# A fused attention and long-convolution kernel: zero products on TensorE at the start, shorter spectrum scaling, and a new order of small steps

## The chip, the cores and the metric

The kernel runs on one core of a Trainium2 chip. Its time is device microseconds (us) from launch to end, lower is better; the kernel before takes 284.23 us (median of 3 runs, 284.17 to 284.6). The engines are named as in the profile: PE is TensorE's matrix products (PEld its weight loads), DVE is VectorE, ACT is ScalarE, POOL is GpSimd, SP is SyncE, which here only issues DMAs. Each engine works its instructions off in the order in which they were written, and waits for the others by semaphores.

## The reference

Two parts, one behind the other. The first is block-sparse attention over 4 batches of 8 heads, 768 positions, 64 channels:

```python
k_rep = k.reshape(B, H, 12, 64, D).mean(axis=3)          # block means of the keys
gate  = einsum('bhsd,bhnd->bhsn', q, k_rep)               # causal blocks only
# each query sees its 3 best blocks and its own block, causally
attn  = softmax(mask(q @ k.T / sqrt(D)))
out   = attn @ v
```

The heads are laid side by side (512 channels) into `x`, and the second part is a gated convolution:

```python
x1, x2, x3 = split(x @ w_proj, 3)
x2_conv = irfft(rfft(x2) * rfft(filter))    # along the 768 positions
y = (x1 * x2_conv * x3) @ w_out
```

## The kernel before, in words

A head (32 in all, n = 0 to 31) is worked in three slots s = 0, 1, 2. A slot issues, in the order written: `scores(n, s)` (L464, products of queries and keys into a two-bank PSUM tile `sps`, then the exponential on ScalarE, L467); in slot 1 `normalise(n - 1)` (L505, L506 on VectorE); in slot 2 of even heads `turn_outputs` (L516, PE turns two heads' outputs `xn` into `xp`, and ScalarE copies them, L518); the stores of finished rows; `diagonals` (L475, Pool zeroes what lies above the diagonal); what the previous slot's unit left for later (`todo`, mostly two products or sums on Pool: L574 and L575 for `PQ`, L612 and L613 for `yT`); `prepare(n, s)` for later heads; `setup`; the units of the convolution of a batch that is finished; and at the end `product(pn, ps)` of the slot before (L490, exponentials times values). Since the order of each engine is the order of writing, it is this sequence that sets what waits behind what.

`prepare` readies heads to come. Up to head 11 queries and keys are cast, and turned on PE (`turn_pe`, L395, copied out at L397 by ScalarE or VectorE); from head 12 they are turned by a DMA on SP's queue (`turn_query`, L384), which waits until `low_query` (L379, Pool) has written the queries' low half from the remainder `rem` that VectorE takes (L375, in `query_rest`). `gate` makes the choice of blocks: products `gps` on PE (L414), then VectorE from L417 to L427 (`ga`, `g`, `m`, `get`, `gm`), and `turn_mask` (L438, L440) turns the result into twelve rows of the queries. Block sums of the keys come from PE for heads below 12 (`key_sums_mm`, L275; `key_sums_copy`, L282 and L284; `key_sums_turn`, L291; `key_sums_split`, L305 and L307). For heads 12 to 31 they come from three lists in `by_block`: DMAs on Pool's queue that add the keys up in memory (`add_blocks`, L319, tile `k_blk`; the last number of each list says in which heads' slot 2 they are issued), a fold and sums on VectorE (`fold_blocks`, L325; `sum_blocks`, L331 and L335, tile `krb`), a turn on PE (`turn_blocks`, L340, tile `krt`) and `split_blocks`.

The start, before head 0, makes the sines of the transform: PE multiplies two short rows into phases (`phase_mm`, L204, tile `dftp`), VectorE rounds (`phase_round`, L209), Pool takes off (`phase_turns`, L215), VectorE adds (`sines`, L223), ScalarE takes the sine (L224). Between these stand the first casts (L364, L357), remainders, turns, key sums and gates of heads 0 and 1, written out by hand. The orders in heads 0 and 1 are in `prepare_first`.

The filter's spectrum is made once, in three parts j: `filter_spectrum` (heads 6, 7, 10, slot 0; L689 and L692, six products into two one-bank PSUM tiles `hspa` and `hspb`, copied out by ScalarE at L696 and L697), then `spectrum_a` and `spectrum_b`, in which `put` scales one of the two by a sine on VectorE (L702) and joins it with the other (L703). There are four one-bank PSUM buffers in all for everything but scores.

The convolution's units for a batch are `unit_x2` (L546, the middle projection), `unit_f1` (transform; VectorE multiplies by the spectrum from L566 to L571, and leaves the sums `PQ` for later on Pool), `unit_x13` (L585 to L590, tile `gx`), `unit_f2` (inverse, `f2a` and `f2b` from L598 on, L604 to L607, and `yT` for later) and `unit_out` (L620, L623).

Of the kernel before, what the change touches and what calls it, by code (L numbers as in the profile page):

```python
# [17 lines left out]
def kernel(  # L18
# [666 lines left out]
    def filter_spectrum(j):  # L685
        sl = slice(P * j, P * (j + 1))
        hc, hs_ = pair("hsp", Dm)
        for i in range(HC):
            nc.tensor.matmul(hc, lhsT=FC[:, i, sl], rhs=fil[:, 0, i, :],  # L689
                             start=(i == 0), stop=(i == HC - 1))  # L690
        for i in range(HC):
            nc.tensor.matmul(hs_, lhsT=FS[:, i, sl], rhs=fil[:, 1, i, :],  # L692
                             start=(i == 0), stop=(i == HC - 1))
# [3 lines left out]
        nc.scalar.copy(hss, hs_)  # L697
        spectra[j] = hcs, hss

    def put(dst, first, s0, second, s1, op):  # L700
        t = p2b.tile([P, Dm], FP32, name="turn", tag="t3", bufs=1)
        nc.vector.tensor_scalar(t, in0=second, scalar1=s1, scalar2=None, op0=ALU.mult)  # L702
        nc.vector.scalar_tensor_tensor(out=dst, in0=first, scalar=s0, in1=t,  # L703
                                       op0=ALU.mult, op1=op)

    def spectrum_a(j):
        hcs, hss = spectra[j]
        put(Asb[:, j, :], hcs, tw[:, 0, j:j + 1], hss, tw[:, 1, j:j + 1], ALU.add)
        if j == 0:
            put(A2, hcs, tw0[:, 0:1], hss, tw0[:, 1:2], ALU.add)  # L710

    def spectrum_b(j):
        hcs, hss = spectra[j]
        cosB = tw0[:, 0:1] if j == 0 else tw[:, 0, j:j + 1]
        put(Bsb[:, j, :], hss, cosB, hcs, tw[:, 1, j:j + 1], ALU.subtract)

# [20 lines left out]
    for fn, slots in ((spectrum_a, ((6, 2), (7, 2), (11, 0))), (spectrum_b, ((7, 0), (8, 0), (11, 1)))):  # L737
        for i, (n, s) in enumerate(slots):
            at(n, s, fn, i)
    for i in range(2):  # L740
# [44 lines left out]
    key_sums_turn(0)  # L785
    turn_pe(0, 0, nc.scalar.copy)
    sines(1)
# [22 lines left out]
    def ready_query(m):  # L810
        if m < PE_HEADS:
            split_query(m)
            cast_key(m)
        else:
            query_rest(m)
        low_query(m)
# [5 lines left out]
    def prepare(n, s):  # L822
# [12 lines left out]
        elif s == 0:  # L835
            if n % 2 == 1 and n + 1 < PE_HEADS:
                turn_mask([n + 1, n + 2], [nc.scalar.copy] * 2)
            if n + 2 in group_at:
                key_sums_turn(group_at[n + 2])
                key_sums_split(group_at[n + 2])  # L840
            for j, group in enumerate(by_block):
                if n + 2 == group[0]:
                    split_blocks(j)
            if n + 4 < NH:
                ready_query(n + 4)
            for j, group in enumerate(by_block):
                if n + 3 == group[0]:
                    fold_blocks(j)
        elif s == 1:
            if PE_HEADS <= n + 4 < NH:  # L850
                turn_query(n + 4)
# [9 lines left out]
        else:  # L861
            for j, group in enumerate(by_block):
                if n + 3 == group[0]:
                    turn_blocks(j)
            if n + 4 < PE_HEADS:
# [13 lines left out]
    def prepare_first(n, s):  # L879
        if (n, s) == (0, 0):  # L880
            gate([1])
            key_mask(2)
            ready_query(2)
            key_sums_mm(2, range(SC))
        elif (n, s) == (0, 1):
            turn_mask([1], [nc.scalar.copy])
            key_sums_copy(2)
            key_sums_turn(2)
            turn_both(2)
            key_sums_split(2)  # L890
            ready_query(3)
            for i in range(1, NB):
# [5 lines left out]
        elif (n, s) == (1, 0):  # L898
            gate([2, 3])
            turn_both(4)  # L900
        elif (n, s) == (1, 1):
            ready_query(5)
# [4 lines left out]
        else:  # L907
            turn_mask([2, 3], [nc.scalar.copy] * 2)
            turn_both(5)
            cast_value(2)  # L910
# [3 lines left out]
    for slot in range(max(units) + 1):  # L914
# [15 lines left out]
        if n < NH:  # L930
            diagonals(n, s)
        for fn in todo:
            fn()
# [4 lines left out]
        for b, fn, *args in units.get(slot, []):  # L938
# [45 lines left out]
```

## Time and profile before

| | |
|---|---|
| median of 3 runs | 284.23 us (284.17 to 284.6) |
| the profiled execution's own time | 283.55 us |
| its span, first to last instruction | 281.8 us |
| mean granted TensorE clock | 0.957 |
| busy: PE, DVE, ACT, POOL | 242.2, 200.5, 182.8, 172.7 us |
| DMA | 41.05 MB, mean 146 GB/s |
| first exponential of head 0, 1, 2, 3 | 13.88, 22.87, 31.19, 37.47 us |

The profile is of one execution. Its busy times are of engines, not of the path; the chain of work that ended last says what the end hung on, and the view of waits says which engine stood idle, and for whom. The granted clock is the share of TensorE's full clock that was let through; it changes in steps between 0.5 and 1.00. A row of the timeline has start and length in us, engine, line, operation, out<-in, and in brackets the idle time before it.

### The profile page before, as it was taken

Reading aid. Unit: us, or ns where it says so; the run is one execution under the profiler, and the core shown is the slowest. Engines: PE = TensorE matmul, PEld = TensorE weight load, DVE = VectorE, ACT = ScalarE, POOL = GpSimd, SP = SyncE. Lnnn points to the kernel's source line nnn. Section 1 sums busy time; section 2 is a strip of 40 time slices with the busy share of each in tenths; the row PEclk is TensorE's granted clock in tenths of the full one; section 3 lists DMA queues with packets and bytes.
Section 4 is the critical chain, followed back from the end, with each engine's and each line's share of the span. In section 5 each row is a group of like instructions: output and inputs, shape, how many; then the busy total and the mean of one; then the engine's idle time right before and its main releaser. Section 6 shows DMA issues by size and latency. Waiting matters only on the chain.

```text
span 281.8 us, 6279 instructions
## 1 busy us (share of the span) xinstructions
PE 242.2 (86%) x2205; PEld 147.6 (52%) x2205; DVE 200.5 (71%) x598; ACT 182.8 (65%) x283; POOL 172.7 (61%) x326
## 2 busy tenths in 40 slices
PE   5878698997799888697999785997999999999994
PEld 3656464654445554365555452664555566455541
DVE  7676659798857999676587865856787843679640
ACT  4656786697658666476687572886776687432454
POOL 7445656676534898397656875675657676408430
PEclk9997979999689999799799997999999999999999
DMA  9998639896795999949999999199673201000046
GB/s 169 218 186 235 148 84 179 151 183 116 136 235 104 181 144 185 207 88 232 173 182 176 210 154 237 28 224 235 135 166 90 69 37 40 37 37 2 1 167 243
DMA packets 115232, 41.05 MB, mean 146 GB/s; under 512 B 107328, under 2 KB 110400, under 8 KB 115200
## 3 DMA queue, kind: packets, MB, share of 16 engines
q1 hardware_dynamic: 110880, 34.61, 60.4%
q0 software_dynamic: 4320, 6.03, 13.5%
q8 instruction: 17, 0.28, 0.4%
q14 instruction: 15, 0.12, 0.1%
HBM read 28.57 MB, written 6.29 MB: 124 GB/s over the span
## 4 chain that ended last, share of the span: by engine, by line
PE 43%; DVE 16%; POOL 12%; ACT 12%; DMA 8%; issue 7%; SPq 0%; ACTq 0%; DVEq 0%; POOLq 0%
ACT ex L467 7%; PE op L620 6%; PE sps L464 6%; DMA qkT<-qk 5%; POOL ex L475 5%; PE o L490 4%; PE x2a L546 4%; PE x2b L546 3%; PE tp L395 3%; DMA k_blk<-in_k_dram 2%; PE x13b L585 2%; PE f2b L601 2%; PE krp L275 2%; POOL PQ L574 2%; POOL PQ L575 2%
## 5 line engine op out<-in xcount | busy, mean ns | idle before, releaser
L467 ACT ACTIVATE ex<-sps 128x1024 f16<-128x1024 f32 (+2 forms) x96 | 87.4, 917 | 53.8 <-PE sps L464 48.8
L475 POOL TENSOR_SCALAR_AFFINE_SELECT ex<-ex 128x128 f16<-128x128 f16 (+1 forms) x128 | 49.2, 401 | 72.5 <-ACT ex L467 70.9
L464 PE MATMUL sps<-qkT 76*128 76x384 f16 (+2 forms) x288 | 55.1, 302 | 0.0
L490 PEld LDWEIGHTS <-ex 128*128 128x128 f16 x672 | 33.1, 100 | 20.9 <-issue 5.2
L490 PE MATMUL o<-v,ex 128*128 128x65 f16 x672 | 37.7, 197 | 2.9 <-POOL ex L475 2.9
L585 PEld LDWEIGHTS <-wp 128*128 128x128 f16 x256 | 24.5, 97 | 22.3 <-issue 8.6
L585 PE MATMUL x13b<-xT,wp 128*128 128x384 f16 x108 | 22.4, 330 | 5.0 <-DVE gx L590 3.4
L464 PEld LDWEIGHTS <-qkT 76*128 76x128 f16 x288 | 21.3, 101 | 5.1 <-issue 1.1
L620 PE MATMUL op<-wo,yT 128*128 128x512 f16 x96 | 23.0, 379 | 0.0
L585 PE MATMUL x13a<-xT,wp 128*128 128x384 f16 x108 | 22.0, 325 | 0.8 <-DVE gx L590 0.8
L613 POOL TENSOR_TENSOR yT<-gx,yy 128x384 f16<-128x384 f32 x16 | 17.2, 1078 | 8.2 <-DVE yy L607 8.2
L574 POOL TENSOR_TENSOR PQ<-t,t 128x512 f16<-128x512 f32 x12 | 16.4, 1369 | 7.5 <-DVE t L567 7.5
L623 ACT COPY osb<-op 128x512 f32<-128x512 f32 x24 | 14.0, 584 | 8.6 <-PE op L620 8.2
L379 POOL TENSOR_SCALAR qk<-rem 128x320 f16<-128x320 f32 x32 | 15.4, 481 | 6.8 <-DVE rem L375 4.4
L506 DVE TENSOR_TENSOR xn<-o,rz 128x384 f16<-128x384 f32 x32 | 17.8, 557 | 1.1
L590 DVE TENSOR_TENSOR gx<-x1sb,x13b 128x384 f32<-128x384 f16 x27 | 14.9, 551 | 5.2 <-ACT x1sb L589 2.5
L395 PE MATMUL tp<-id_f,qk 128*76 128x128 f16 (+1 forms) x144 | 13.5, 245 | 5.0 <-POOL qk L379 1.4
L375 DVE TENSOR_TENSOR rem<-q_nat,qk 128x320 f32<-128x320 f32 x32 | 17.0, 532 | 1.0
L401 POOL CAST v<-v_nat 128x384 f16<-128x384 f32 x32 | 16.4, 512 | 1.0 <-DMA v_nat<-in_v_dram 0.9
L357 POOL CAST qk<-k_nat 128x384 f16<-128x384 f32 x31 | 16.2, 522 | 0.0
L440 ACT COPY qkT<-gmp 12x640 f16<-12x640 f16 x22 | 15.0, 680 | 1.2 <-PE gmp L438 0.7
L546 PEld LDWEIGHTS <-xT 128*128 128x128 f16 x96 | 9.9, 105 | 11.0 <-issue 2.6
(151 smaller groups left out, 491.4 us busy)
## 6 DMA issues: line engine op xcount, KB each, us to landing
q_nat<-in_q_dram SPq DMA_DIRECT2D x32, 192.0 KB, 4.2
k_nat<-in_k_dram SPq DMA_DIRECT2D x32, 192.0 KB, 4.3
v_nat<-in_v_dram SPq DMA_DIRECT2D x32, 192.0 KB, 4.2
out_dram<-osb SPq DMA_DIRECT2D x24, 256.0 KB, 2.1
k_blk<-in_k_dram POOLq DMA_DIRECT2D x10, 384.0 KB, 6.0
rows<-in_moe_filter_fft_dram SPq DMA_DIRECT2D x2, 768.0 KB, 6.6
wp<-in_moe_w_proj_dram POOLq DMA_DIRECT2D x6, 256.0 KB, 4.9
wo<-in_moe_w_out_dram POOLq DMA_DIRECT2D x2, 256.0 KB, 9.1
```

The costliest lines, as they stand in the source:

```text
L375: nc.vector.tensor_sub(rems[n], q_nat[:, 1:SC], qk16[:, 0, 1:SC, 0:D])
L395: nc.tensor.transpose(tp[0:rows_, P * c:P * (c + 1)], qk16s[n % NB][:, t, c, 0:rows_], id_f16)
L464: nc.tensor.matmul(sps[:, col:col + qe - qs], lhsT=turned[n][0:76, 1, kc, :], rhs=qT[0:76, qs:qe], start=True, stop=True, skip_group_check ...
L467: nc.scalar.activation(ex[:, lo:hi], sps[:, lo:hi], AF.Exp, bias=0.0, scale=scale)
L475: nc.gpsimd.affine_select(out=sub, in_=sub, compare_op=ALU.is_ge, fill=0.0, base=0, pattern=[[0, cnt], [1, P]], channel_multiplier=-1)
L490: nc.tensor.matmul(outs[n][:, qc * DE:(qc + 1) * DE], lhsT=ex[:, col + P * j:col + P * (j + 1)], rhs=vals[n][:, kc, 0:DE], start=(gi == 0 ...
L506: nc.vector.tensor_tensor(out=xns[n // 2][:, :, D * (n % 2):D * (n % 2 + 1)], in0=o[:, :, 0:D], in1=rz.to_broadcast([P, SC, D]), op=ALU.mult)
L546: nc.tensor.matmul(pp, lhsT=xT[:, dc, base + P * i:base + P * (i + 1)], rhs=wp[:, dc, Dm:2 * Dm], start=(dc == 0), stop=(dc == DC - 1))
L574: nc.gpsimd.tensor_sub(PQ[:, 0, j, :], t1, t2)
L585: nc.tensor.matmul(dst, lhsT=wp[:, dc2, base:base + P], rhs=xT[:, dc2, hs:hs + HALF], start=(dc2 == 0), stop=(dc2 == DC - 1))
L613: nc.gpsimd.tensor_mul(yT[:, dc, S - 1:HALF - 1:-1], st["g"][:, dc, 1, :], yy[:, 1, :])
L620: nc.tensor.matmul(op, lhsT=yT[:, cc, P * scn:P * (scn + 1)], rhs=wo[:, cc, :], start=(cc == 0), stop=(cc == DC - 1))
```

## The change

- `warm(times)` is new: products of a tile of zeros (`gm16s[1]`, 128 by 128) with zeros (512 columns) into the second half of the tile `dftp` of the second phase, which nobody reads. Five stand behind the three phases, two behind the turns of head 0, two behind head 1's key sums.
- Head 0's queries are copied out of PSUM by VectorE instead of ScalarE. Head 1's queries are turned behind head 0's first scores, head 3 is made ready before head 2 is turned, head 4 is turned a slot later and head 5 two slots later (in head 2).
- The spectrum's parts are made in heads 6, 8, 10. ScalarE scales by the sine as it copies out of PSUM; VectorE only joins, reading the other tile from PSUM, in slot 1 of the same heads.
- `query_rest` and `low_query` for heads from 12 on stand before `todo`, so ahead of the two Pool operations left by the previous slot's unit.
- The third list of `by_block` is issued in heads 13, 15, 17, 19 instead of 14, 16, 18, 20. `turn_blocks` stands behind the slot's units instead of ahead of them.

The core of the diff:

```diff
-    by_block = [(12, 4, 2, [6, 7]), (16, 8, 1, [8, 9, 10, 11]), (24, 8, 1, [14, 16, 18, 20])]
+    by_block = [(12, 4, 2, [6, 7]), (16, 8, 1, [8, 9, 10, 11]), (24, 8, 1, [13, 15, 17, 19])]
...
-        hcs = p2b.tile([P, Dm], FP32, name="hcs", tag="hcs")
-        hss = p2b.tile([P, Dm], FP32, name="hss", tag="hss")
-        nc.scalar.copy(hcs, hc)
-        nc.scalar.copy(hss, hs_)
-        spectra[j] = hcs, hss
+        scaled = []
+        for name, src, w in (("hss", hs_, tw[:, 1, j:j + 1]), ("hcs", hc, tw[:, 1, j:j + 1]),
+                             ("hs0", hs_, tw0[:, 1:2]))[:3 if j == 0 else 2]:
+            scaled.append(p2b.tile([P, Dm], FP32, name=name, tag=name, bufs=1))
+            nc.scalar.mul(scaled[-1], src, w)
+        spectra[j] = hc, hs_, scaled
...
+    def spectrum(j):
+        hc, hs_, scaled = spectra.pop(j)
+        cosB = tw0[:, 0:1] if j == 0 else tw[:, 0, j:j + 1]
+        nc.vector.scalar_tensor_tensor(out=Asb[:, j, :], in0=hc, scalar=tw[:, 0, j:j + 1],
+                                       in1=scaled[0], op0=ALU.mult, op1=ALU.add)
+        nc.vector.scalar_tensor_tensor(out=Bsb[:, j, :], in0=hs_, scalar=cosB,
+                                       in1=scaled[1], op0=ALU.mult, op1=ALU.subtract)
         if j == 0:
...
+            nc.vector.scalar_tensor_tensor(out=A2, in0=hc, scalar=tw0[:, 0:1],
+                                           in1=scaled[2], op0=ALU.mult, op1=ALU.add)
...
-    for i, n in enumerate((6, 7, 10)):
+    for i, n in enumerate((6, 8, 10)):
         at(n, 0, filter_spectrum, i)
...
+    def warm(times):
+
+        for _ in range(times):
+            nc.tensor.matmul(phases["big", 1][:, 512:1024], lhsT=gm16s[1][:, 1, :],
+                             rhs=gm16s[1][:, 2:SC, :].rearrange("p c s -> p (c s)"),
+                             start=True, stop=True, skip_group_check=True)
...
     for i in range(HC):
         phase_mm(i)
+    warm(5)
...
-    turn_pe(0, 0, nc.scalar.copy)
+    turn_pe(0, 0, nc.vector.tensor_copy)
+    warm(2)
...
     key_sums_mm(1, range(SC))
+    warm(2)
     turn_mask([0], [nc.scalar.copy])
...
     turn_pe(1, 1, nc.vector.tensor_copy)
     key_sums_split(1)
-    turn_pe(1, 0, nc.vector.tensor_copy)
...
+            if n == 2:
+                turn_both(5)
...
-            if n + 4 < NH:
+            if n + 4 < PE_HEADS:
                 ready_query(n + 4)
...
+            if n in (6, 8, 10):
+                spectrum(n // 2 - 3)
...
         if (n, s) == (0, 0):
+            turn_pe(1, 0, nc.vector.tensor_copy)
             gate([1])
...
             turn_mask([1], [nc.scalar.copy])
+            ready_query(3)
             key_sums_copy(2)
...
         elif (n, s) == (1, 0):
             gate([2, 3])
+        elif (n, s) == (1, 1):
             turn_both(4)
-        elif (n, s) == (1, 1):
             ready_query(5)
...
             diagonals(n, s)
+            if s == 0 and PE_HEADS <= n + 4 < NH:
+                query_rest(n + 4)
+                low_query(n + 4)
         for fn in todo:
             fn()
...
-        if s == 2 and PE_HEADS <= n + 5 < NH:
-            cast_query(n + 5, nc.scalar.copy)
+        if s == 2:
+            if PE_HEADS <= n + 5 < NH:
+                cast_query(n + 5, nc.scalar.copy)
+            for j, group in enumerate(by_block):
+                if n + 3 == group[0]:
+                    turn_blocks(j)
```

More of the change, by code (lines that the diff above doesn't have):

```diff
@@ L693, in filter_spectrum @@
                              start=(i == 0), stop=(i == HC - 1))
-        hcs = p2b.tile([P, Dm], FP32, name="hcs", tag="hcs")
-        hss = p2b.tile([P, Dm], FP32, name="hss", tag="hss")
-        nc.scalar.copy(hcs, hc)
-        nc.scalar.copy(hss, hs_)
-        spectra[j] = hcs, hss
[L700 to L708, printed above, removed]
-        if j == 0:
[L710 to L715, printed above, removed]
+        scaled = []
[11 more added lines that the diff above has]
+                                       in1=scaled[1], op0=ALU.mult, op1=ALU.subtract)
+        if j == 0:
+            nc.vector.scalar_tensor_tensor(out=A2, in0=hc, scalar=tw0[:, 0:1],
+                                           in1=scaled[2], op0=ALU.mult, op1=ALU.add)
     def weights(dst, src, cols, ns):
@@ L810, in ready_query @@
     def ready_query(m):
[L811 to L815, printed above, removed]
+        split_query(m)
+        cast_key(m)
         low_query(m)
```

8 lines of the change are left out of this document (removed).

## The prediction, as it was written before the changed kernel ran

> **What bounds the kernel now.** I read the page first: its busy shares, the granted clock in slices, and the shares of the chain that ended last.
>
> ```profile
> PE 242.2 (86%) x2205; PEld 147.6 (52%) x2205; DVE 200.5 (71%) x598; ACT 182.8 (65%) x283; POOL 172.7 (61%) x326
> ...
> PEclk9997979999689999799799997999999999999999
> ...
> PE 43%; DVE 16%; POOL 12%; ACT 12%; DMA 8%; issue 7%; SPq 0%; ACTq 0%; DVEq 0%; POOLq 0%
> ```
>
> PE is busy 86% of 281.8 us and holds only 43% of the chain: PE is the engine to feed, and the other half of the chain is what it waits for. The slices under 9 in the clock row say when its clock was cut. So two things are worth money: PE's waits, and the spells at half clock. The view of waits, summed by engine, has the long single ones:
>
> ```profile
> PE gps L414 <- DMA qkT<-qk: 4.2, 4, 1.4
> ...
> DVE k_blk L325 <- DMA k_blk<-in_k_dram: 3.6, 1, 3.6
> PE x13b L585 <- DVE gx L590: 3.4, 1, 3.4
> ...
> PE krt L340 <- DVE krb L335: 2.7, 2, 2.0
> ```
>
> Columns: total us, times, longest. The second and third are one event: VectorE waits 3.6 for the block sums' last load, and PE 3.4 behind it. Then the granted clock, in stretches of 3.41 us cut where it changes (columns: length, busy us of PE, PEld, DVE, ACT, POOL, granted clock, DMA):
>
> ```profile
> 22.02:25.44 3.42, 3.42 (x35) 2.40 (x32) 2.17 (x15) 2.48 (x3) 2.00 (x5) 0.50 0.76 186
> 69.81:73.22 3.41, 2.15 (x32) 1.26 (x31) 3.30 (x8) 2.09 (x4) 1.96 (x4) 1.00 0.73 120
> 73.22:76.64 3.42, 2.63 (x23) 2.06 (x24) 3.25 (x19) 2.36 (x5) 1.91 (x5) 0.50 0.78 133
> 110.77:114.18 3.41, 1.52 (x14) 0.66 (x13) 3.24 (x8) 2.06 (x4) 3.26 (x6) 1.00 1.06 211
> 114.18:117.60 3.42, 3.23 (x18) 2.00 (x19) 1.41 (x4) 0.89 (x2) 0.67 (x2) 0.50 1.19 219
> 131.25:134.66 3.41, 1.69 (x24) 1.21 (x25) 2.31 (x16) 1.91 (x3) 3.23 (x6) 1.00 1.15 234
> 134.66:138.08 3.42, 3.22 (x17) 1.79 (x17) 1.81 (x5) 2.09 (x5) 1.58 (x3) 0.50 1.11 163
> 168.80:172.21 3.41, 0.19 (x2) 0.12 (x2) 1.36 (x4) 1.09 (x2) 3.16 (x5) 1.00 1.08 241
> 172.21:175.62 3.41, 3.33 (x19) 1.63 (x18) 2.56 (x7) 0.81 (x1) 0.26 (x2) 0.50 1.16 228
> ```
>
> The four half-clock stretches whose forerunner is shown follow one in which PE was busy 0.19 to 2.15 of 3.41 us. So a stall is paid twice: its own length, and then half of the 3.2 to 3.4 busy us behind it, 1.6, because they ran at half clock.
>
> **The change part by part.**
>
> *Low halves first on Pool.* For heads 16 up, the low half of the next queries (L379) stands on Pool behind the previous unit's two products. The chain in order of time:
>
> ```profile
> 125.26 0.97 POOL yT L612
> ...
> 127.28 0.45 POOL qk L379
> 127.76 4.86 DMA qkT<-qk
> ...
> 154.36 1.27 POOL PQ L575
> ...
> 155.72 0.45 POOL qk L379
> 156.20 4.81 DMA qkT<-qk
> ```
>
> The transpose (SP's queue) starts as soon as L379 ends and takes 4.8 to 4.9 us; the gate's products on PE wait for its landing four times, 4.2 in all by the view of waits. With L379 ahead of the two products it ends about 2 us sooner (1.00 twice, or 1.27 and about 0.9), more than any of the waits (longest 1.4). So they go: 4.2, of which I keep **3.6**, since the ScalarE copies behind them can be late next. Bounds 2 and 4.2. The price is 0.45 us on the two products, which other units use a slot or more later.
>
> *Block sums a head earlier* (heads 13, 15, 17, 19 for 14, 16, 18, 20).
>
> ```profile
> 164.45 6.34 DMA k_blk<-in_k_dram
> ```
>
> The last load is issued at 164.45, lands 6.34 later, and VectorE's fold in head 21 had nothing to do meanwhile. A head is 6 to 8 us here, so a load one head earlier has landed. PE's 3.4 go; I count **3.2**, bounds 2 and 3.4. The number of loads and Pool issues is unchanged.
>
> *Turning the block sums at the end of the slot.* PE stands still at krt 2.7 us in two heads:
>
> ```profile
> 111.47 1.26 POOL L575 TENSOR_TENSOR PQ<-t,t 128x512 f16<-128x512 f32 x1
> ...
> 114.37 0.39 PE L340 MATMUL krt<-id_f,krb 96*128 96x96 f32 x1 [1.96 <-DVE krb L335]
> ...
> 114.56 1.17 PE L598 MATMUL f2a<-inv,PQ 128*128 128x384 f16 x3
> ```
>
> Behind it, f2a needs only PQ, done at 112.73; with the low half now ahead of PQ on Pool, at about 113.2. So f2a starts 1.3 sooner, and head 9's 0.7 goes: **2.0**, bounds 0.7 and 2.7.
>
> *Spectrum.* It loses seven scalings on VectorE and keeps seven joins (L703), which now read PSUM and are taken at the same 0.82:
>
> ```profile
> L703 DVE SCALAR_TENSOR_TENSOR Bsb<-hss,tw,turn 128x512 f16<-128x512 f32 x3 | 2.5, 817 | 0.1
> ...
> L702 DVE TENSOR_SCALAR turn<-hss,tw 128x512 f32<-128x512 f32 x4 | 2.3, 574 | 0.0
> ...
> L702 DVE TENSOR_SCALAR turn<-hcs,tw 128x512 f32<-128x512 f32 x3 | 2.0, 676 | 0.0
> ...
> L697 ACT COPY hss<-hspb 128x512 f32<-128x512 f32 x3 | 1.8, 585 | 0.4 <-PE hspb L692 0.3
> ```
>
> VectorE is relieved of 2.3 + 2.0 = 4.3; ScalarE gets one copy-sized operation more (0.59; the scaled ones are taken at the copy's 585 ns). But the joins, three of 0.82 in head 6 and two in heads 8 and 10, now stand together ahead of the gate, and hold two PSUM banks that the transposes of the outputs (xp) of the same head need: PE's xp now waits for the joins. In head 6 that is:
>
> ```profile
> 58.23 0.56 DVE L506 TENSOR_TENSOR xn<-o,rz 128x384 f16<-128x384 f32 x1
> ...
> 59.00 0.33 PE L516 MATMUL xp<-id_f,xn 128*128 128x128 f16 x3
> ```
>
> The joins would run 58.8 to 61.3, so xp waits from 59.0 to 60.5 and its second half to 61.3: about 2 us late at the end of head 6. Heads 7 and 8, where VectorE is full (3.30 of 3.41 in the row of 69.81 above), lose five of the seven scalings, some 3.1 us of VectorE, and get it back. Net **+1.0**, bounds: a loss of 5.7 (seven joins of 0.82 all on the path) and a gain of 4.3.
>
> *Zero products and the start.* Rows of the first 15 us:
>
> ```profile
> 1.97 1.11 PE L204 MATMUL dftp<-fsin,tvals 1*128 1x384 f16 x3 [1.97 <-POOL fsin L139]
> ...
> 3.12 1.49 DVE L209 TENSOR_SCALAR dft_ka<-dftp 128x384 f32<-128x384 f32 x3 [0.66 <-PE dftp L204]
> ...
> 7.77 0.80 ACT L397 COPY qkT<-tp 128x768 f16<-128x768 f16 x1 [0.17 <-PE tp L395]
> ...
> 7.90 0.55 DVE L223 TENSOR_TENSOR dftp<-dftp,dft_ka 128x384 f32<-128x384 f32 x1
> ...
> 9.04 0.22 DVE L417 TENSOR_TENSOR ga<-gps,cbias 128x60 f32<-128x60 f32 x1 [0.59 <-PE gps L414]
> ...
> 13.88 1.02 ACT L467 ACTIVATE ex<-sps 128x1024 f16<-128x1024 f32 x1 [1.75 <-PE sps L464]
> ```
>
> and a 512-column product at half and at full clock, from the chain:
>
> ```profile
> 78.46 1.72 PE x2b L546 x4
> ...
> 140.28 0.86 PE x2a L546 x4
> ```
>
> 0.43 against 0.21 each. The three phases run at the slow price: 1.11 for three of 384 columns is 0.37 each, where 0.43 for 512 columns makes 0.32 and 0.21 makes 0.16; so the chip starts at half clock, whatever the clock row says of its first slices. Five zero products behind the three phases so take 3.0 to 5.2. They write the tile of the second phase, and in the changed program the second rounding (L209) waits for all five: it starts at 5.2, not 3.6, and VectorE is 1.6 late with all that follows. Then head 0's query copy goes to VectorE (0.55 for ScalarE's 0.80), ending at about 9.9 for 8.57; and behind it two L223 (0.55 each) and three smaller steps, which used to run while the gate waited, now stand ahead of it, by estimate 2 us in all: the gate starts at about 12.0, not 9.04. I count the first exponential at 15.5 to 16.0, not 13.88. What is got back: scores (0,0) no longer wait for head 1's query transposes, heads 3 to 5 are turned at other places, and PE may be at full clock where it was cut (22.02 to 25.44 above, 3.42 busy us, worth 1.7). Net at head 3: **1.0 lost**; bounds 3.0 lost and 1.5 gained. Whether products of zeros lift the clock no row of this trace shows.
>
> *Clock.* The three cut stretches from 110 on stand right behind the three stalls that go. Two of them saved, one new one elsewhere: **+1.6**; bounds 0 and 4.8.
>
> *Sum.* 3.6 + 3.2 + 2.0 + 1.0 + 1.6 - 1.0 = 10.4 us. The profiled execution's own time is 283.55 (span 281.8 and 1.7 around it), 0.7 under the median 284.23; the saving is taken off the median: **273.8 us**.
>
> A rule weighed: the Trainium skill, "TensorE: Matmul & The Clock Gate", section "HAM oscillation — how this bites in real kernels", says the clock falls for idle gaps of PE over about 3.4 us. The rows differ: the stretch 110.77 to 114.18 had 1.96 as its longest gap, and the clock fell. By the rule only the stall of 3.4 at 168.6 takes the clock away, the cut stretches of 114.18 and 134.66 stay, and rival 1, worth 3.2 by them, is out of reach; the forecast itself, which counts one stretch net, stands. Since the rows show the clock falling behind shorter gaps, rival 1 keeps its chance.
>
> **Rivals.**
> 1. *The clock stays whole and the start is repaid* (chance 0.20): all three stretches go with no new one (3.2 more) and the start nets nothing (1.0 more): 269.6. For it: the cut follows half-idle stretches only. Against: every shift of work makes new half-idle ones.
> 2. *The start keeps its delay* (0.10): VectorE is the chain from 14 to 20 us, nothing is repaid, 3.0 lost instead of 1.0, and zeros do not count for the clock, one more cut stretch (1.6): 277.4.
> 3. *Clock unmoved, half the waits return* (0.15): other cut stretches appear (1.6 less) and half of 3.6 + 2.0 turns into waits for ScalarE or Pool (2.8 less): 278.2. The row of POOL 3.26 in 110.77:114.18 speaks for it.
> 4. *Slower: the held banks* (0.05): each join stands on PE's path in heads 6, 8 and 10 (5.7) and each of the three stalls cuts the clock behind it (4.8). In place of +1.0 that is 10.5 lost: 273.8 + 1.0 + 10.5 = 285.3. It decides if VectorE is over 2 us behind PE when xp is due in all three heads; against it, heads 7 and 11 have their VectorE work taken away.
> 5. *The stalls are not what they seem* (0.03): the changed order meets a like wait elsewhere and nothing is left: 284.2.
>
> **How the numbers follow.** The forecast has 0.47, its own range 271 to 277. A measurement of this kernel can tell about 0.2%, 0.6 us, from no change. Faster: 0.47 + 0.20 + 0.10 + 0.15 = 0.92; same 0.03; slower 0.05. The range leaves out less than 2 in 10: 268.5, a little under rival 1, to 279.5, over rivals 2 and 3.
>
> **What would show it.** Right: no wait of gps for the transpose over 0.5 us, none of k_blk for its load, no 2 us wait before krt, three fewer cut stretches after 110, L702's group gone from VectorE. For the start: second rounding at 5.2, first gate at about 12, first exponential at 15.5 to 16. Wrong: xp waiting over 2 us in each of heads 6, 8 and 10; head 3's first exponential over 2 us later than 37.5; cut stretches as many as before.

## The result, and the profile after

| | before | changed |
|---|---|---|
| median of the timed runs | 284.42 us (284.17 to 290.13, 4 runs) | **270.47 us** (268.72 to 271.14, 4 runs) |
| the profiled execution's own time, and its span | 283.55, 281.8 us | 268.72, 267.0 us |
| mean granted clock of that execution | 0.957 | 0.980 |

The ratio is 0.9503 [0.9441, 0.9565]: faster by 14 us, where 10.4 were forecast. On another chip (run c_after below) the same kernel took 268.56 us beside 283.62. The ratios leave disturbed runs of the kernel before out, and so are not the quotients of the medians.

The page of the changed kernel, the same three rows as were shown of before:

```profile
PE 237.2 (89%) x2214; PEld 144.5 (54%) x2214; DVE 197.8 (74%) x592; ACT 182.1 (68%) x283; POOL 170.4 (64%) x326
...
PEclk9897999999999999979999999999999999999999
...
PE 45%; DVE 22%; ACT 15%; POOL 7%; issue 7%; DMA 3%; SPq 0%; ACTq 0%; POOLq 0%; DVEq 0%
```

PE has nine products more and is busy 5.0 us less; it had three stretches at half clock instead of seven (below). From 30 us on the clock row has one dip where before had five. In the chain DMA fell from 8% to 3% and Pool from 12% to 7%: those were the transposes, the block sums and what stood ahead of them on Pool. VectorE rose from 16% to 22%; it is what stands next to PE now.

The view of waits (total us, times, longest):

```profile
PE krt L340 <- DVE krb L335: 2.1, 2, 1.0
...
DVE dft_ka L209 <- PE dftp L755: 1.7, 1, 1.7
...
PE x13b L585 <- DVE t L570: 1.7, 3, 0.7
```

The row of gps waiting for the transposes (4.2 before) is gone, and so are VectorE's wait for the last load of block sums (3.6) and PE's behind it (3.4). krt still waits twice, 1.0 each, where its longest was 2.0: in head 13, and now in head 21, where it had not waited before. The second row is new: the rounding that waits for the zero products.

Stretches of the granted clock (columns as before: length, busy us of PE, PEld, DVE, ACT, POOL, clock, DMA):

```profile
3.98:7.39 3.41, 3.41 (x22) 1.97 (x20) 1.99 (x5) 1.02 (x2) 1.55 (x4) 1.00 1.33 225
7.39:10.80 3.41, 1.42 (x16) 0.77 (x14) 2.58 (x9) 1.66 (x3) 2.80 (x10) 1.00 1.37 218
10.80:14.22 3.42, 3.42 (x26) 2.12 (x23) 2.17 (x13) 2.19 (x4) 1.04 (x3) 0.50 1.33 218
21.04:24.46 3.42, 3.42 (x35) 3.12 (x34) 1.39 (x4) 1.61 (x2) 0.41 (x3) 0.50 0.87 226
109.79:113.20 3.41, 1.88 (x31) 1.44 (x31) 3.31 (x10) 1.79 (x3) 2.07 (x6) 1.00 1.14 244
113.20:116.62 3.42, 3.28 (x22) 2.12 (x22) 2.80 (x15) 1.98 (x5) 3.25 (x6) 0.50 0.80 177
```

The three rows at 0.50 are all the cuts of this execution before its last microseconds. Before had seven, of which six came after 30 us: from 35.7, two from 73.2 to 80.1, and from 114.2, 134.7 and 172.2. One cut is left in the neighbourhood of the one at 114.2: the one at 113.2.

The first exponential of a head tells where time was won. Both columns are starts in the profiled executions (L467 on ScalarE), and the gain is their difference:

| head | before, us | changed, us | gained so far |
|---|---|---|---|
| 0 | 13.88 | 15.26 | -1.38 |
| 3 | 37.47 | 37.61 | -0.14 |
| 7 | 61.73 | 62.61 | -0.88 |
| 10 | 86.60 | 82.13 | 4.47 |
| 13 | 107.73 | 103.28 | 4.45 |
| 14 | 117.92 | 111.44 | 6.48 |
| 17 | 137.32 | 129.19 | 8.13 |
| 21 | 165.67 | 155.44 | 10.23 |
| 22 | 177.02 | 163.49 | 13.53 |
| 31 | 234.38 | 219.50 | 14.88 |

### The profile page after: what moved, and what is told of

It is laid out like the page before. It is cut to its first block, busy times and chain, and to the rows that moved or that the text cites. A ratio compares the mean times of both kernels' runs of the same rounds, so it can differ in the third digit from the quotient of the medians.

```text
span 267.0 us, 6284 instructions
## 1 busy us (share of the span) xinstructions
PE 237.2 (89%) x2214; PEld 144.5 (54%) x2214; DVE 197.8 (74%) x592; ACT 182.1 (68%) x283; POOL 170.4 (64%) x326
## 3 DMA queue, kind: packets, MB, share of 16 engines
q0 software_dynamic: 4320, 6.03, 14.2%
## 4 chain that ended last, share of the span: by engine, by line
PE 45%; DVE 22%; ACT 15%; POOL 7%; issue 7%; DMA 3%; SPq 0%; ACTq 0%; POOLq 0%; DVEq 0%
ACT ex L467 7%; PE sps L464 6%; PE op L620 6%; PE o L490 4%; PE x13b L585 4%; POOL ex L475 3%; DMA q_nat<-in_q_dram 3%; PE x2a L546 3%; PE x2b L546 3%; ACT qkT L440 3%; DVE t L570 3%; DVE t L567 2%; PE f2b L601 2%; PE krp L275 2%; DVE m L423 2%
## 5 line engine op out<-in xcount | busy, mean ns | idle before, releaser
L467 ACT ACTIVATE ex<-sps 128x1024 f16<-128x1024 f32 (+2 forms) x96 | 87.3, 918 | 44.1 <-PE sps L464 38.7
L475 POOL TENSOR_SCALAR_AFFINE_SELECT ex<-ex 128x128 f16<-128x128 f16 (+1 forms) x128 | 47.8, 387 | 58.1 <-ACT ex L467 57.2
L464 PE MATMUL sps<-qkT 76*128 76x384 f16 (+2 forms) x288 | 53.0, 292 | 0.5 <-ACT qkT L440 0.5
L490 PEld LDWEIGHTS <-ex 128*128 128x128 f16 x672 | 32.4, 99 | 20.6 <-issue 6.0
L490 PE MATMUL o<-v,ex 128*128 128x65 f16 x672 | 36.9, 195 | 3.6 <-POOL ex L475 0.9
L585 PEld LDWEIGHTS <-wp 128*128 128x128 f16 x256 | 24.5, 97 | 18.1 <-issue 4.4
L585 PE MATMUL x13b<-xT,wp 128*128 128x384 f16 x108 | 21.9, 325 | 2.2 <-DVE t L570 1.7
L464 PEld LDWEIGHTS <-qkT 76*128 76x128 f16 x288 | 20.6, 98 | 5.2 <-issue 0.8
L585 PE MATMUL x13a<-xT,wp 128*128 128x384 f16 x108 | 22.0, 325 | 0.0
L574 POOL TENSOR_TENSOR PQ<-t,t 128x512 f16<-128x512 f32 x12 | 15.3, 1271 | 8.1 <-DVE t L567 7.5
L590 DVE TENSOR_TENSOR gx<-x1sb,x13b 128x384 f32<-128x384 f16 x27 | 14.9, 551 | 5.8 <-ACT x1sb L589 4.8
L575 POOL TENSOR_TENSOR PQ<-t,t 128x512 f16<-128x512 f32 x12 | 15.2, 1268 | 0.0
L546 PEld LDWEIGHTS <-xT 128*128 128x128 f16 x96 | 9.2, 97 | 9.6
```

The source lines that it names most:

```text
L464: nc.tensor.matmul(sps[:, col:col + qe - qs], lhsT=turned[n][0:76, 1, kc, :], rhs=qT[0:76, qs:qe], start=True, stop=True, skip_group_check ...
L467: nc.scalar.activation(ex[:, lo:hi], sps[:, lo:hi], AF.Exp, bias=0.0, scale=scale)
L475: nc.gpsimd.affine_select(out=sub, in_=sub, compare_op=ALU.is_ge, fill=0.0, base=0, pattern=[[0, cnt], [1, P]], channel_multiplier=-1)
L490: nc.tensor.matmul(outs[n][:, qc * DE:(qc + 1) * DE], lhsT=ex[:, col + P * j:col + P * (j + 1)], rhs=vals[n][:, kc, 0:DE], start=(gi == 0 ...
L546: nc.tensor.matmul(pp, lhsT=xT[:, dc, base + P * i:base + P * (i + 1)], rhs=wp[:, dc, Dm:2 * Dm], start=(dc == 0), stop=(dc == DC - 1))
L585: nc.tensor.matmul(dst, lhsT=wp[:, dc2, base:base + P], rhs=xT[:, dc2, hs:hs + HALF], start=(dc2 == 0), stop=(dc2 == DC - 1))
```

## The experiments

They ran in three groups, each on a chip of its own beside the kernel before: a_late_blocks, a_low_behind, a_no_zero and a_own_bank (before 286.11 us there, 279.15 to 291.3), a_old_spectrum, a_turn_ahead, a_old_heads and b_fill (284.46, 279.08 to 289.26), and the four whose names begin with c_ or are b_zero (283.62, 278.8 to 289.12). The changed kernel itself differs by 1.9 us between two occasions, so of medians from different groups only more than that counts. The traces say more: the exponentials of a_late_blocks, a_turn_ahead and a_old_spectrum start within 0.05 us of the changed kernel's up to the head in which the programs differ, and those of a_low_behind run up to 0.4 ahead of it. Below, "head 7 takes 5.1 us" means from its first exponential to that of head 8.

### The last block sums a head later again (a_late_blocks)

```diff
-    by_block = [..., (24, 8, 1, [13, 15, 17, 19])]
+    by_block = [..., (24, 8, 1, [14, 16, 18, 20])]
```

> The changed kernel with the third list of block loads back in heads 14, 16, 18, 20. Theory (a stall of PE costs its own length and half of the stretch behind it): the 3.4 us wait in head 21 is back and a cut stretch behind it, 3.4 + 1.6: 275.5 us. Rival, lengths alone: 273.9. Rival, the load is hidden in the new order anyway: 270.5.

274.95 us (273.48 to 275.38, 4 runs), near the 275.5 of the theory. Its waits, and its clock at head 21:

```profile
PE x13b L585 <- DVE gx L590: 3.4, 1, 3.4
...
DVE k_blk L325 <- DMA k_blk<-in_k_dram: 3.2, 1, 3.2
...
PE gps L414 <- DMA qkT<-qk: 1.7, 1, 1.7
```

```profile
160.90:164.30 3.40, 0.70 (x6) 0.44 (x6) 2.27 (x5) 0.55 (x2) 2.80 (x4) 1.00 1.25 227
164.30:167.70 3.40, 3.40 (x24) 2.08 (x23) 2.28 (x7) 1.70 (x3) 0.75 (x2) 0.50 0.85 158
```

Up to head 20 its exponentials lie within 0.05 us of the changed kernel's (148.81 against 148.85). The wait is back with its old length of 3.4, a cut stretch stands right behind it, and head 22 begins at 168.44 instead of 163.49. But these 4.95 us are not the one stall and its clock. Head 21 already begins 1.78 late (157.22 against 155.44), behind a second wait that came back: in head 20 the gate waits 1.66 for a transpose that was issued at 146.45 instead of 145.12 and took 6.1 us to land. Head 21 itself loses 3.17, although its stall is 3.44 and a cut stretch follows, because the wait of 1.04 at krt, which the changed kernel has in this head, does not come. So 3.44 less 1.04 are waits, and by this estimate about 0.8 is left for the cut stretch, not 1.6. The theory's sum was near for another reason than its own.

### The queries' remainders and low halves behind what the units leave again, heads 16 and on (a_low_behind)

```diff
-            if s == 0 and PE_HEADS <= n + 4 < NH:
-                query_rest(n + 4)
-                low_query(n + 4)
...
             if n + 4 < PE_HEADS:
                 ready_query(n + 4)
+            elif n + 4 < NH:
+                query_rest(n + 4)
+                low_query(n + 4)
```

> The changed kernel with the low half of heads 16 up back behind the two Pool operations that a unit leaves. Theory: three waits of the gate's products for the transpose are back, 1.2 to 1.45 each, 4.1 in all, and one cut stretch, 1.6: 276.2 us. Rival, lengths alone: 274.6. Rival, the transposes are no longer late since the heads start at other times: 270.5.

277.08 us (276.1 to 278.38, 4 runs). The row of waits that had gone is back:

```profile
PE gps L414 <- DMA qkT<-qk: 4.8, 4, 2.1
```

And the clock is cut where it was whole:

```profile
103.20:106.60 3.40, 3.40 (x17) 1.68 (x16) 2.85 (x11) 1.22 (x4) 0.75 (x2) 0.50 1.27 211
...
116.80:123.70 6.90, 6.10 (x42) 3.95 (x43) 3.37 (x17) 3.23 (x6) 3.30 (x7) 0.51 1.09 218
```

Head 13 begins at 106.88 instead of 103.28, head 15 at 122.90 instead of 117.72. Taken back, this part costs the most: 6.6 us by the medians, 7.4 by the two spans (274.4 against 267.0). About half of that is head 12, which takes 4.0 us more. There PE waits 1.05 for a transpose and 1.52 for `gx` of VectorE, and VectorE was held up by one remainder:

```profile
97.39 3.72 DVE L375 TENSOR_TENSOR rem<-q_nat,qk 128x320 f32<-128x320 f32 x1
...
98.12 1.40 POOL L574 TENSOR_TENSOR PQ<-t,t 128x512 f16<-128x512 f32 x1
...
99.35 1.39 POOL L575 TENSOR_TENSOR PQ<-t,t 128x512 f16<-128x512 f32 x1
```

It takes 3.72 us where the median is 0.49, and ends 0.36 behind the end of Pool's second product. In the changed order the low half, which needs the remainder, stands ahead of the two products, so the two cannot meet; in none of the ten profiled executions of that order do they, and there no remainder of these heads takes over 1.27. From head 13 on a_low_behind loses 3.8, close to the prediction's 3.6.

### The block sums turned ahead of the slot's units again (a_turn_ahead)

```diff
         else:
+            for j, group in enumerate(by_block):
+                if n + 3 == group[0]:
+                    turn_blocks(j)
             if n + 4 < PE_HEADS:
...
-            for j, group in enumerate(by_block):
-                if n + 3 == group[0]:
-                    turn_blocks(j)
```

> The changed kernel with the block sums turned ahead of the slot's units again. Theory: PE waits at krt 1.3 us longer in head 13, 0.7 in head 9 and about as much in head 21: 2.5 in all, 273.0 us, and 1.6 more if a cut stretch follows. Rival, krt waits 1 us behind the units too, so the place matters little: 271.

272.36 us (272.21 to 274.13, 4 runs), ratio to before 0.9604 [0.9553, 0.9656]. Its row of krt:

```profile
PE krt L340 <- DVE krb L335: 5.3, 3, 2.3
```

Against the changed kernel's 2.1 that is 3.2 us more, and it is paid in the heads of the three turns: 0.72 at head 9, 1.0 more at head 13 and 2.1 more at head 21. In head 14 it gains 0.8, for the cut stretch at 113.2 does not come here; one at 164.3, behind the turn of head 21, does. The rest is spread. The profiled pair ends 3.7 us apart, the medians 1.9.

### The spectrum as it was (a_old_spectrum)

```diff
-    for i, n in enumerate((6, 8, 10)):
+    for i, n in enumerate((6, 7, 10)):
         at(n, 0, filter_spectrum, i)
...
-            if n in (6, 8, 10):
-                spectrum(n // 2 - 3)
```

with `put`, `spectrum_a`, `spectrum_b` and their slots as before.

> The changed kernel with the spectrum as it was (copies on ScalarE, scalings and joins on VectorE, heads 6, 7 and 10, spread over slots). Theory: VectorE binds heads 7 and 8 again and PE waits there, which cuts the clock behind it; heads 6 to 10 take 26.4 us in the changed kernel and 30.4 before, 0.7 of that is krt, so 3.3 are lost: 273.8 us. Rival, the prediction's own size of the step (net 1.0, since the held banks take most of it back): 271.5. Rival, no gain: 270.5 or less.

271.6 us (270.72 to 272.96, 4 runs), ratio 0.9568 [0.9515, 0.962]. Start for start it is the changed kernel up to head 6 (55.70 in both). Head 7 then begins at 61.23 instead of 62.61, so the new joins do cost 1.4 us in head 6; but head 8 begins at 69.52 instead of 67.67 and head 10 at 85.03 instead of 82.13. Its stretches there:

```profile
68.76:72.17 3.41, 2.42 (x42) 1.51 (x39) 3.27 (x9) 2.44 (x4) 1.67 (x5) 1.00 0.68 112
72.17:75.58 3.41, 2.37 (x21) 1.68 (x21) 3.24 (x18) 2.18 (x5) 2.27 (x5) 0.50 0.88 137
75.58:79.00 3.42, 3.42 (x13) 1.50 (x12) 0.73 (x2) 2.88 (x4) 1.23 (x3) 0.50 1.00 218
```

VectorE has no room (3.27 and 3.24 of 3.41), PE waits behind it, and the two cut stretches of before are back at nearly the same place. In the profiled pair the new spectrum gains 3.1 at the end; by the medians only 1.1. So the median lies at the rival of 271.5, the prediction's own size of the step, and not at the theory's 273.8; but 1.1 is inside what groups differ by. More traces help: heads 6 to 9 take 26.4 us in nine of ten profiled executions with the new spectrum (27.15 in a_turn_ahead, whose krt waits there), and 28.7 to 30.4 in the four with the old one, of which 0.7 is krt in three. The tenth, c_no_zero, had two cut stretches there and took 29.06.

### Heads 0 to 2 in the old order, with the zero products (a_old_heads)

```diff
-    turn_pe(0, 0, nc.vector.tensor_copy)
+    turn_pe(0, 0, nc.scalar.copy)
     warm(2)
```

and the turns and preparations of heads 1, 3, 4 and 5 at their old places.

> The changed kernel with the old order of heads 0 to 2 and ScalarE's copy of head 0's queries; the zero products stay. Theory: the second rounding is as late (5.4), the first gate at 10.5 to 11 for 11.3, but heads 1 and 2 are slower by about 2, so head 3 stands 1 us later than 37.6: 271.5. Rival, the copy on VectorE is what delays the start and the old order is as good: 269.5.

271.67 us (271.27 to 272.21, 4 runs), ratio 0.9571 [0.9525, 0.9618]. Head 0 begins at 16.48 instead of 15.26 and head 3 at 39.14 instead of 37.61: the new order, with the copy on VectorE, wins 1.5 us by head 3. Part of it may be the clock's, which is cut from 10.1 to 20.4 here, and from 10.8 to 14.2 and 21.0 to 24.5 in the changed kernel. Another 1.1 is lost in head 4, where a cut stretch begins at 47.7.

### Without the zero products, twice (a_no_zero, c_no_zero and c_after)

```diff
-    warm(5)
...
-    warm(2)
...
-    warm(2)
```

> The changed kernel without the nine zero products. Theory: they cost VectorE 1.6 us at the second rounding and give back a faster PE from 7 to 11 us, so about nothing: 270.5, between 269.5 and 271.5; the second rounding starts at 3.6 and the first gate about 1.5 sooner than 11.3. Rival, the zero products carry the change (the clock from the start decides the rest): 280 or more.

268.02 us (267.13 to 268.54, 4 runs), under the 269.5 to 271.5 expected. The rival, by which the products carry the change, falls: without them nothing is lost. Rows of the timeline of a_no_zero:

```profile
3.12 1.49 DVE L209 TENSOR_SCALAR dft_ka<-dftp 128x384 f32<-128x384 f32 x3 [0.66 <-PE dftp L204]
...
10.13 0.21 DVE L417 TENSOR_TENSOR ga<-gps,cbias 128x60 f32<-128x60 f32 x1
...
14.49 1.02 ACT L467 ACTIVATE ex<-sps 128x1024 f16<-128x1024 f32 x1 [1.17 <-PE sps L464]
...
18.66 0.93 PE L464 MATMUL sps<-qkT 76*128 76x384 f16 x3
```

And the same of the changed kernel:

```profile
3.01 2.31 PE L755 MATMUL dftp<-gm 128*128 128x512 f16 x5
...
3.12 0.56 DVE L209 TENSOR_SCALAR dft_ka<-dftp 128x384 f32<-128x384 f32 x1 [0.66 <-PE dftp L204]
...
5.36 1.02 DVE L209 TENSOR_SCALAR dft_ka<-dftp 128x384 f32<-128x384 f32 x2 [1.69 <-PE dftp L755]
...
11.34 0.20 DVE L417 TENSOR_TENSOR ga<-gps,cbias 128x60 f32<-128x60 f32 x1
...
15.26 1.02 ACT L467 ACTIVATE ex<-sps 128x1024 f16<-128x1024 f32 x1 [0.68 <-PE sps L464]
...
17.84 0.55 PE L464 MATMUL sps<-qkT 76*128 76x384 f16 x3
```

The zero products do lift the clock: three products of scores take 0.55 us with them and 0.93 without. But they hold the second rounding back by 1.7 us, the first choice of blocks comes 1.2 later, and by head 3 the two are level (37.61 and 37.35). To settle the 2 us of the medians, the two ran again side by side, with the next one:

> The changed kernel once more, unaltered, to stand beside the next two on the same chip. Its four runs so far lay between 268.7 and 271.1 us with a median of 270.5; I expect 269 to 271. If it falls under 268.5, the earlier difference of about 2.5 us to the kernel without the zero products was one of chips and occasions, and not of the products.

> The changed kernel without its nine zero products, a second time. Theory: the second rounding waits for the five products and VectorE hands its lateness on, while the full clock that they bring forward lasts one stretch and is cut again before the first scores; so without them it is 1.5 to 3 us faster than the changed kernel of the same job, 267 to 268.5. Rival: the two are level within 0.7 us, and the earlier difference was chance in where the cut stretches fell.

The changed kernel took 268.56 us (267.59 to 269.47, 6 runs; 0.9565 [0.9514, 0.9617]), the one without zero products 267.15 (266.59 to 269.74, 6 runs; 0.9523 [0.9465, 0.958]). The medians differ by 1.4 in the same direction, but the runs overlap and so do the intervals: no run speaks for a gain by the zero products, that they cost 1 to 2 us is likely, and no more. The profiled execution of c_no_zero was its slowest. It was ahead at head 3 (35.90, c_after 37.24), and lost that again in heads 6, 7 and 9, where its clock was cut and that of a_no_zero, the same program, was not:

```profile
73.54:76.95 3.41, 3.41 (x13) 1.49 (x13) 0.83 (x2) 2.02 (x4) 1.77 (x3) 0.50 1.07 222
```

Head 9, in which this one lies, took 10.44 us, and 8.76 in a_no_zero.

### The five zero products in a PSUM bank of their own (a_own_bank)

```diff
-    warm(5)
+    warm(5, one_tile("warm"))
```

`warm` takes the tile to write to; the other four products stay as they were.

> The changed kernel with its first five zero products written to a PSUM bank of their own, so that the second rounding does not wait for them. Theory: rounding at 3.6 for 5.36, VectorE and with it the first gate 1.5 sooner, the first exponential 1.0 to 1.5 sooner than 15.26, and most of it kept: 269.3. Rival, the start is absorbed by head 3 whatever it is: 270.5.

267.47 us (266.77 to 268.96, 4 runs), level with the kernel without them, and faster than theory and rival said. The three roundings run in one row again, but the first choice still begins at 11.11, the first exponential at 15.29 and head 3 at 38.44 (37.61 in the changed kernel), so no gain in the start is seen:

```profile
3.12 1.49 DVE L209 TENSOR_SCALAR dft_ka<-dftp 128x384 f32<-128x384 f32 x3 [0.66 <-PE dftp L204]
...
11.11 0.21 DVE L417 TENSOR_TENSOR ga<-gps,cbias 128x60 f32<-128x60 f32 x1
```

```profile
12.50:26.10 13.60, 12.74 (x94) 9.29 (x95) 7.53 (x28) 6.33 (x8) 4.58 (x12) 0.50 0.83 172
```

The clock that was lifted was cut again from 12.5 to 26.1. So the bank is not all that the products cost in the start. The two behind head 0's turns still go to the old tile, and VectorE's L223 waits 0.31 for them at 9.36; the rest is not traced.

### Without zero products, head 0's queries copied by ScalarE (c_scalar)

```diff
-    warm(5)
...
-    turn_pe(0, 0, nc.vector.tensor_copy)
-    warm(2)
+    turn_pe(0, 0, nc.scalar.copy)
...
-    warm(2)
```

> The changed kernel without the zero products, and with head 0's queries copied out by ScalarE again, as before the change. If VectorE is what the first gate waits for, taking 0.55 us of copying from it brings the first exponential from about 14.5 to about 14.0 and the end forward by up to 0.5 us: 267.0 to 268.0, a little under the kernel without zero products. Rival: head 0 to 3 are bound by the order that follows, head 3's first exponential stays at 37.3 to 37.4, and the time is level with that kernel within 0.4 us.

267.18 us (265.79 to 268.54, 6 runs), ratio 0.9522 [0.9457, 0.9586]. Its first exponential came at 13.43, a full 1.0 before c_no_zero's 14.43, and head 3 at 35.13 against 35.90; the medians are level within 0.1. So the rival is right in the time, though not in head 3 (37.3 to 37.4 expected). The lead in the trace says little: a_no_zero, the same program as c_no_zero, had head 3 at 37.35.

### The zero products alone, in the kernel before (b_zero)

```diff
         phase_mm(i)
+    warm(5)
...
     turn_pe(0, 0, nc.scalar.copy)
+    warm(2)
...
     key_sums_mm(1, range(SC))
+    warm(2)
```

> The kernel before with the nine zero products alone, at the same three places, and nothing else of the change. Theory: they lift the clock early (full from about 7 us instead of 15), but the second rounding is 1.5 us late, so that the first exponential comes 1 to 2 us later than 13.88 and the whole is 0 to 2.5 us slower than the kernel before: 284 to 287. Rival: the earlier clock pays in heads 0 and 1, where stretches were cut, and the whole is 1 to 2 us faster: 282 to 283.

286.24 us (284.1 to 288.33, 6 runs), ratio 1.0199 [1.0121, 1.0277]: slower, though its runs lie within the 278.8 to 289.12 of the kernel before beside it. The first exponential comes 2.6 later (13.88 before), more than the 1 to 2 expected:

```profile
16.47 1.02 ACT L467 ACTIVATE ex<-sps 128x1024 f16<-128x1024 f32 x1 [1.75 <-PE sps L464]
```

```profile
9.60:19.90 10.30, 9.21 (x61) 5.86 (x61) 7.60 (x33) 4.32 (x7) 3.93 (x13) 0.50 0.98 155
```

The full clock that the products brought forward was gone from 9.6 to 19.9, up to and over the first scores.

### The kernel before, with its waits filled by zero products (b_fill)

The waits stay, but PE works while it waits, so that its clock isn't cut behind them: 7 products of 512 columns ahead of krt in head 13, 10 of 256 between the two halves of the gate of heads 18, 22 and 26 (worked in heads 16, 20 and 24), and 36 of 128 ahead of x13b in head 21.

```diff
+        fill(krt, 512, {1: 7}.get(j, 0))
...
+            if h == 1 and ns[0] in (18, 22, 26):
+                fill(gpt[:, 256:512], 256, 10)
...
+            if slot == 64 and base >= 2 * Dm:
+                fill(x1f[:, HALF:512], P, 36)
```

> The kernel before, with products of zeros that nobody reads put on PE where it waits: ahead of krt in head 13 (7 of 512 columns, about 1.5 us at full clock), between the two halves of the gate's products of heads 18, 22 and 26 (10 of 256, 1.1 us each), and ahead of x13b in head 21 (36 of 128, about 2 us). The waits last as long as before. Theory (the clock is cut because PE was half idle in the stretch ahead): the cut stretches behind 114, 134 and 172 do not come, 1.6 each: 4.8 less than the kernel before. Rival, zeros do not count as work, or the clock does not hang on the stalls: no change, or up to 1 us more.

285.65 us (283.58 to 292.44, 10 runs), ratio 1.013 [1.0061, 1.0198]. The theory's 4.8 us do not come, though the clock of the profiled execution was 0.981, as high as the changed kernel's 0.980; its span is 284.4. Of the three stretches named two are gone, and one begins at 133.4. The row, and waits (its L424, L347, L340, L500, L598 and L603 are L414, L340, L335, L490, L585 and L590 of before):

```profile
PEclk9999999999799979998899999999999999999999
```

```profile
PE gps L424 <- DMA qkT<-qk: 5.5, 4, 2.3
...
PE o L500 <- DVE gx L603: 2.4, 1, 2.4
...
PE x13b L598 <- DVE gx L603: 1.7, 1, 1.7
...
PE krt L347 <- DVE krb L340: 1.4, 2, 0.7
```

The wait of 2.4 is not the fillers': it stands in head 12, and the first of them in head 13. Ahead of it a remainder of VectorE again took 3.54 us for 0.49, under Pool's two products as in a_low_behind, and head 12 took 10.37 us for 7.08. From head 13 on, where all fillers stand, the kernel took 129.4 us, and 126.7 before, with one cut stretch instead of three. PE waited less before krt (1.4 in all for 2.7) and x13b (1.7 for 3.4), and longer in the gate (5.5 for 4.2); heads 16, 20 and 24, in which the gate's fillers stand, took 1.4, 2.0 and 0.7 more. So with the fillers in place the fuller clock won no time. The fillers' own length stands on the path as well, and how much of the loss is theirs, this run doesn't separate.

## Why the prediction was right, and where it was off

The time fell inside the range and the sign was right; the forecast of 273.8 was 3.3 us high (5.2 beside the second chip), and the time came close to rival 1 (269.6). The profiled pair saved 14.83 us (283.55 less 268.72) against 10.4. Of the signs that were to show it right, one failed: two cut stretches fewer after 110 us, not three. The 0.6 us that a measurement was to tell from no change was too small: the kernel before ran from 279 to 291 us in the groups that followed. By its own terms:

**From head 13 on: right in the sum, less so in the parts.** Low halves 3.6, block sums 3.2, the part of `turn_blocks` in head 13 1.3, clock 1.6: 9.7 in all. The table gives 14.88 - 4.45 = 10.4. The blocks: head 21 gains 13.53 - 10.23 = 3.3, but by some luck, for the wait of 3.4 and the cut stretch behind it are gone, and the new wait of 1.04 at krt, which the prediction did not have, is paid. The transposes: no wait is left of 4.2, and heads 16, 20 and 24 gain 2.4, 1.6 and 1.4, the first with its cut stretch. The turn in head 13: 2.0, of which 0.8 is given back in head 14, where the cut stretch of 113.2 now lies. Which clock share belongs to which is not to be had, since these runs bring cuts back with their waits.

**The low halves were worth more than their wait.** Taken back alone they cost 6.6 to 7.4, not 3.6. The waits for transposes came back not only where they were (in a_low_behind PE waits 1.05 us in head 12 and 2.09 in head 14, where before hardly waited), and in head 12 the long remainder stands with them; how often it comes in other executions is not known. That the new order keeps remainder and products apart, the prediction did not see. The parts' prices, each taken out alone, do not add up to the whole: the five of them come to 21.6 us by the spans, where the whole change brings 14.8.

**The spectrum: the direction was right, a part of the return was left out.** This is the step that failed: "Net **+1.0**", where the profiled pair shows 3.3 and a_old_spectrum 2.9 between heads 6 and 10. The cost in head 6 was foreseen as about 2 and was 1.4 in a_old_spectrum; of the joins and of the waits for them the changed kernel shows

```profile
58.56 0.75 DVE L705 SCALAR_TENSOR_TENSOR Asb<-hspa,tw,hss 128x512 f16<-128x512 f32 x1 [0.28 <-ACT hcs L699]
...
59.89 0.74 DVE L710 SCALAR_TENSOR_TENSOR A<-hspa,tw,hs 128x512 f16<-128x512 f32 x1
60.02 0.33 PE L516 MATMUL xp<-id_f,xn 128*128 128x128 f16 x3 [0.86 <-DVE Bsb L707]
...
60.68 0.33 PE L516 MATMUL xp<-flip,xn 128*128 128x128 f16 x3 [0.33 <-DVE A L710]
```

The return was taken as the 3.1 us of scalings in heads 7 and 8. But joins stood there too, and they also left. Before, head 7 had four scalings (2.15 us) and these three joins, and has none of them now:

```profile
62.78 1.01 DVE L703 SCALAR_TENSOR_TENSOR Asb<-hcs,tw,turn 128x512 f16<-128x512 f32 x1
...
64.37 0.87 DVE L703 SCALAR_TENSOR_TENSOR A<-hcs,tw,turn 128x512 f16<-128x512 f32 x1
...
66.54 0.82 DVE L703 SCALAR_TENSOR_TENSOR Bsb<-hss,tw,turn 128x512 f16<-128x512 f32 x1
```

So the joins that cost 1.4 in head 6 are joins that head 7 no longer has; the prediction counted their cost and not their return. Head 7 alone gains 3.2 (8.29 us before, 5.06 now), ahead of the two cut stretches, which makes 1.8 net with head 6. Heads 8 and 9 gain 2.1 more. Of that 0.7 is the wait of head 9's turn, and at most the other 1.4 is the clock's: the two cut stretches from 73.2 to 80.1 went, and a_old_spectrum brought them back. The prediction had quoted the first of them, and then counted in its clock term only "the three cut stretches from 110 on". No row of the waits is long there; a sum of single long waits has no place for them.

**The clock: less than one price per stretch.** Forecast: two saved, one new, 1.6 net. The trace: of six cuts behind 30 us one is left, and c_after, the same program, has none after 25:

```profile
110.29:113.70 3.41, 2.37 (x44) 1.75 (x41) 3.27 (x12) 1.83 (x2) 1.90 (x5) 1.00 0.97 233
113.70:117.12 3.42, 2.83 (x28) 1.80 (x26) 3.31 (x15) 2.80 (x6) 3.34 (x6) 1.00 1.12 168
```

There the stretch of 113 stayed whole, and head 15 began at 116.68 against 117.72, 0.6 of it won since head 14. So one stretch cost 0.6 here, about 0.8 by estimate behind the block sums (a_late_blocks) and 1.7 in head 9 of c_no_zero; in the kernel with filled waits, fewer of them gained nothing. The price of 1.6 is near the top of what was seen and not the rule. Why it differs was not tested; that the next wait takes up a part, as that of krt did in head 21 of a_late_blocks, fits.

**The start: right in the chain, too dark in the net.** Foreseen were the second rounding at 5.2, the first choice at about 12, the first exponential at 15.5 to 16.0, and 1.0 lost by head 3; measured 5.36, 11.34, 15.26 and 0.14. In the profiled executions the new order wins 1.5 by head 3 (a_old_heads), and the zero products alone lose 1.5 there (b_zero, 38.93 against 37.47). The two nearly cancel; but two executions of one program (a_no_zero, c_no_zero) also lie 1.45 apart at head 3.

**The rivals.** The slower one (held banks) had its wait, 1.2 us in head 6, and missed its deciding point of 2 in all three heads. Rival 1 named nearly the right time with half the reason: the start was repaid, but of the three stretches one stayed; the rest came from the spectrum, which it left at +1.0. The rule of the Trainium skill that was weighed ("TensorE: Matmul & The Clock Gate", section "HAM oscillation — how this bites in real kernels", idle gaps over about 3.4 us) differs from the changed kernel's rows too: the cut at 10.80 follows a stretch in which PE's waits were 0.86 and 1.13 us long.

```profile
8.37 0.23 PE L291 MATMUL krt<-id_f,krs 12*128 12x12 f32 x1 [0.86 <-DVE krs L284]
...
10.60 0.29 PE L414 MATMUL gps<-kr,qkT 128*128 128x24 f16 x5 [1.13 <-DVE kr L307]
```

**A version at least as fast.** Without its zero products the change had medians of 268.02 and 267.15 us, against 270.47 and 268.56 with them, and 267.18 with the copy by ScalarE too; of these only 267.15, 267.18 and 268.56 were measured side by side.

## What to carry to other kernels

A stall of PE costs its length, and a cut stretch behind it cost another 0.6 to 1.7 us in these runs; a wait that moves elsewhere pays some of it back. Take the wait away rather than keep PE busy through it: filling the waits brought the clock and no time. Before a stall is priced from a run that brings it back, look at every head for what else came back. When work is moved, count it where it leaves as well as where it arrives. Products that warm the clock must write where nobody waits, and the clock must stay whole until the work comes; here they won nothing.

## What the runs showed of the hardware that was not expected

Products of zeros count as work for the clock: the first record of full clock is at 7.39 us with them, and at 18.5 to 24.1 in three executions of the change without them. Up to the first record the column says 1.00, yet five 512-column products took 2.31 us, 0.46 each, the price of half clock.

How full PE must be to keep the clock is not one number of busy time: it was cut behind a stretch with 2.42 of 3.41 us busy (a_old_spectrum) and kept behind one with 2.37 (c_after).

A subtraction of two tiles on VectorE (`rem`) took 3.72 and 3.54 us instead of 0.49 in the two places where Pool's two products (`PQ`) ran over it, and ended 0.36 behind the second of them both times.

One and the same program has its cuts at different places from run to run. The stretches of 3.41 us lie differently against its work: in the changed kernel one ends at 113.20, with PE busy 1.88, and the next is cut; in c_after it ends at 113.70, with PE busy 2.37, and the next is whole. Two runs of the kernel before beside c_after took 278.8 us at a mean clock of 0.975 and 282.61 at 0.957, and a difference of 2 us between two such kernels needs more than one run of each.
